# Chunk attention and a GELU feed-forward layer on one core: PSUM banks, AV order and an output copy at the seam between the first two tiles

## The chip, the core and the metric

The kernel runs on one core of one Trainium2 chip. The core has a matrix engine (TensorE, PE in the profile, with PEld for its weight loads), a vector engine (VectorE, DVE), an activation engine (ScalarE, ACT), a general engine (GpSimd, POOL) and SyncE (SP), which here issues nearly all DMAs. Each engine works through its own instructions in program order, and semaphores make one wait for another. Matmuls write to PSUM, which is handed out here as eight banks of 128 partitions x 512 float32.

The metric is the device time of one execution in microseconds (us), smaller is better. Times in the profile's views count from the first instruction of the profiled execution.

## What is computed

Attention within chunks of 64 tokens, for 8 batches, 8 heads, 576 tokens and 64 channels a head; its result, as 4608 rows of 512, goes through a layer 512 -> 2048 -> 512 with the exact GELU.

```
scores = scale * np.matmul(q_c, k_c.transpose(0, 1, 2, 4, 3))     # q_c, k_c, v_c: (8, 8, 9, 64, 64)
attn = np.exp(scores - max);  attn = attn / attn.sum(-1)
x = (attn @ v_c).transpose(0, 2, 1, 3).reshape(4608, 512)
h = x @ w_in                                                       # (4608, 2048)
g = 0.5 * h * (1.0 + erf(h / sqrt(2)))
out = g @ w_out                                                    # (4608, 512)
```

## The kernel before

**Tiles.** The 72 chunk positions are cut into nine tiles of 512 tokens (`NT = 9`): tiles 0 to 7 are the first 512 tokens of a batch each, tile 8 the last chunks of all batches. For each tile the kernel does attention, which leaves `x` (512 channels as four groups of 128 partitions, `G = 4`), then mm1 (`h_ps`, line 298: 16 groups f of four accumulating matmuls, one for each k slice `ks` = channel group of `x`, followed by a Gelu on ACT, line 301), then mm2 (`y_ps`, lines 314 and 349: four row blocks ms of 16 matmuls), whose results are copied to SBUF as `y_sb` (line 318) and written out by a DMA that SP issues (line 323 for tiles 0 to 7).

**Software pipeline.** The order is written by hand and kept (`manual_schedule`). While PE does mm1 and mm2 of tile t, the attention of tile t + 1 is put between, slot by slot, by the dictionaries `extra1` (before mm1 group f) and `extra2` (before mm2 slot s) that `phase` is given. One channel group g (two heads) of attention is: scores on PE and exp on ACT (`att_S`, `pT`); the sums of the exps and their reciprocals; AV, eight matmuls of 64 columns into `av_ps` (line 264); and on DVE the multiplication of `av_ps` by the spread reciprocals `rc` into `x[g]` (line 265).

**Reciprocals.** For tile 1 group 0 has its own path (`att_sum`, lines 200 to 209). Groups 1 to 3 go through `att_sums(1, 1)`: four matmuls (line 218), a transpose and a reciprocal on DVE (lines 221, 223), then 12 small copies on ACT (line 227, four for each g, into `rb`); `att_rc` then makes `rc` of one g from `rb` by a DVE transpose (line 234).

**Tile 0's mm2.** It goes by rows (`by_rows=True`): slots 0 to 11 do one f for all four row blocks at once (`mm2_rows`), so four `y_ps` banks are open: three from the pool `ps_mm` and, for ms = 3, one from `ps_at`. Slots 12 to 15 finish the row blocks ms = 0 to 3 in turn, four matmuls each (`mm2_slot`, qt = 3), and each is then copied to `y_sb`: ms 0 to 2 on ACT, ms 3 on DVE. After ms = 2 ACT loads the Gelu table. In these slots stand the sums of tile 1 (slot 12), AV 0 and `rc` 1 (slot 13), AV 1 and `rc` 2 (slot 15), and AV 2 and `rc` 3 at the end; AV 3 stands in mm1 of tile 1, before its k slice 1 (`between`, `last_av`).

**Tile 1's mm1.** `phase` starts mm1 of a tile with several groups at once (`first`, line 357: 2 for tile 0, 3 for tile 1, 1 for the others), k slice by k slice, so that a late `x[g]` holds up less. For tile 1 these are `h_ps` 0 to 2, all from `ps_mm`.

**Pools.** PSUM is split into `ps_mm` (3 banks: `h_ps`, `y_ps`), `ps_tp` (2) and `ps_at` (3: scores, sums, AV; and `y_ps` 3 of tile 0). For tile 1 AV 0 and 1 are in `ps_at`, AV 2 and 3 in `ps_tp`. A tile gets a bank when its former user is done with it; the banks are assigned when the program is built. `y_sb` has four buffers in turn.

**Queues.** In the loop over tiles, SP issues in program order: the outputs of tile t - 1 (as mm2 produces them), the two transposing DMAs of tile t + 1 (`flip`, line 163, q and k), for t = 1 also the eight v loads of tile 2 (line 129), then q, k and eight v loads of tile t + 2 (lines 112 and 129). POOL casts `v_bd` of tile t + 1 (line 137) and q and k of tile t + 2 (line 133).

Of the kernel before, what the change touches and what calls it, by code (L numbers as in the profile page):

```python
# [11 lines left out]
def kernel(  # L12
# [9 lines left out]
    nc = tc.nc  # L22
    P = 128
    f32 = mybir.dt.float32
    bf16 = mybir.dt.bfloat16
    Act = mybir.ActivationFunctionType

    B, H, S, D = q.shape
    CH = 64
# [3 lines left out]
    G = H // 2  # L33
    d_model = H * D
# [3 lines left out]
    MT = CT * CH  # L38
    NT = B + 1
# [31 lines left out]
    def zero_v(i, eng):  # L71
        eng.memset(v_bds[i][0:CH, :, :, CH:P], 0.0)
        eng.memset(v_bds[i][CH:P, :, :, 0:CH], 0.0)
# [17 lines left out]
    ypool = ctx.enter_context(tc.tile_pool(name="ypool", bufs=4))  # L91
    ps_mm = ctx.enter_context(tc.tile_pool(name="ps_mm", bufs=3, space=bass.MemoryType.PSUM))
    ps_tp = ctx.enter_context(tc.tile_pool(name="ps_tp", bufs=2, space=bass.MemoryType.PSUM))
    ps_at = ctx.enter_context(tc.tile_pool(name="ps_at", bufs=3, space=bass.MemoryType.PSUM))
# [3 lines left out]
    def stage_tile():  # L98
        return stage.tile([P, SW], f32, tag="stage", name="arrival")

    tiles = [dict() for _ in range(NT)]

    def load_qk(t, nm, h0=0, h1=H):

        st = tiles[t]
        src = q if nm == "q" else k
        if nm + "f" not in st:
            st[nm + "f"] = stage_tile()[:].rearrange("p (h j d) -> p h j d", h=H, j=J)
            st[nm] = ld.tile([P, G, J, 2, D], bf16, tag=nm, name=f"{nm}_nat")
        raw = st[nm + "f"]  # L110
        if t < B:
            nc.sync.dma_start(raw[:, h0:h1], src[t, h0:h1, 0:MT, :].rearrange("h (p j) d -> p h j d", j=J))  # L112
        else:
            for b in range(B):
                nc.sync.dma_start(
                    raw[PC * b:PC * (b + 1), h0:h1],
                    src[b, h0:h1, MT:S, :].rearrange("h (p j) d -> p h j d", j=J))
# [29 lines left out]
    def att_Tq(t, g, copy):  # L147
        tp = transposed(t, "q", g)
        qT = work.tile([P, CT, CH], bf16, tag="qT", name="qT", bufs=5)
        copy(qT[:].rearrange("p i (c j) -> p i c j", j=J), tp)  # L150
        tiles[t]["qT", g] = qT
# [59 lines left out]
            return rest_of_it  # L211
        rest_of_it()

    def att_sums(t, first=0):

        sum_ps = ps_at.tile([P, MT], f32, tag="at", name="sums_ps")
        for g in range(G):
            nc.tensor.matmul(sum_ps[QD * g:QD * (g + 1)], ones_c[:], tiles[t]["pT", g][:], start=True, stop=True,  # L218
                             tile_position=(0, QD * g))
        t1 = work.tile([P, NB, 32], f32, tag="t1", name="t1", bufs=2)  # L220
        nc.vector.transpose(t1[:], sum_ps[:].rearrange("p (n e) -> p n e", e=32))  # L221
        r1 = work.tile([P, 2, NB], f32, tag="r1", name="r1", bufs=2)
        nc.vector.reciprocal(r1[:], t1[:].rearrange("p n (r e) -> p r n e", r=2)[:, :, :, 0])  # L223
        rb = work.tile([P, G, NB], f32, tag="rb", name="rb", bufs=2)
        for g in range(first, G):
            for s in range(G):
                nc.scalar.copy(rb[QD * s:QD * (s + 1), g], r1[QD * g:QD * (g + 1), s // 2])  # L227
        tiles[t]["rb"] = rb

    def att_rc(t, g):  # L230

        rb = tiles[t]["rb"]
        rc = work.tile([P, NB, 32], f32, tag="rc", name="rc", bufs=4)
        nc.vector.transpose(rc[:], rb[:, g].to_broadcast([P, NB, 32]))  # L234
        tiles[t]["rc", g] = rc
# [34 lines left out]
    DV, AC, PO = nc.vector.tensor_copy, nc.scalar.copy, nc.gpsimd.tensor_copy  # L270

    def att_units(t, cq=DV, ck=DV):
        tiles[t]["x"] = xpool.tile([P, G, MT], bf16, tag="x", name="x")
        T = []
        for g in range(G):
            T += [lambda g=g: att_Tq(t, g, cq), lambda g=g: att_Tk(t, g, ck if t == 0 or g < 2 else DV)]
        S_ = [lambda g=g: att_S(t, g) for g in range(G)]
        if t > 1:
            T = [lambda g=g: flip_k(t, g, ck) for g in range(G)]
            S_ = [lambda g=g: att_S_flipped(t, g) for g in range(G)]  # L280
        if t > 0:
            U = [lambda: att_sums(t), *[lambda g=g: att_rc(t, g) for g in range(G)]]
        else:
            U = [lambda g=g: att_sum(t, g) for g in range(G)]
        A = [lambda g=g: att_av(t, g) for g in range(G)]
        return T, S_, U, A


    def mm1_slot(t, f, n=1, between={}):
        st = tiles[t]  # L290
        if f == 0:
            st["h"] = hpool.tile([P, FF, MT], bf16, tag="h", name="h")
        h_ps = [ps_mm.tile([P, MT], f32, tag="mm", name="h_ps") for _ in range(n)]
        for ks in range(KS):
            for u in between.get(ks, ()):
                u()
            for a in range(n):
                nc.tensor.matmul(h_ps[a][:], w_in_sb[:, ks, (f + a) * P:(f + a + 1) * P], st["x"][:, ks, :],  # L298
                                 start=(ks == 0), stop=(ks == KS - 1))
        for a in range(n):  # L300
            nc.scalar.activation(st["h"][:, f + a, :], h_ps[a][:], Act.Gelu)  # L301

    NQ = 4
    def mm2_slot(t, ms, qt):
        st = tiles[t]
        if t == NT - 1 and ms == MT // P - 1:
            if qt == 0:
                last_rows(t, ms)
            return
        if qt == 0:  # L310
            st["y_ps", ms] = ps_mm.tile([P, d_model], f32, tag="mm", name="y_ps")
        y_ps = st["y_ps", ms]
        for f in range(qt * FF // NQ, (qt + 1) * FF // NQ):
            nc.tensor.matmul(y_ps[:], st["h"][:, f, ms * P:(ms + 1) * P], w_out_sb[:, f, :],  # L314
                             start=(f == 0), stop=(f == FF - 1))
        if qt == NQ - 1:
            y_sb = ypool.tile([P, d_model], f32, tag="y", name="y_sb")
            (AC if t == 0 and ms < 3 or ms % 2 == 0 and t + 1 < NT else DV)(y_sb[:], y_ps[:])  # L318
            if t == 0 and ms == 2:
                act_table(Act.Gelu)  # L320
            if t < B:
                m0 = t * S + ms * P
                nc.sync.dma_start(out[m0:m0 + P, :], y_sb[:])
            else:
                for c in range(P // CH):
                    m0 = (ms * (P // CH) + c) * S + MT
                    nc.sync.dma_start(out[m0:m0 + CH, :], y_sb[c * CH:(c + 1) * CH, :])

    def last_rows(t, ms):
        h = d_model // 2  # L330
# [21 lines left out]
    def phase(t, extra1, extra2, by_rows=False, between={}):  # L352
        nms = MT // P
        order = [(ms, qt) for ms in range(nms) for qt in range(NQ)]
        if by_rows:
            order = [(None, f) for f in range(FF - FC)] + [(ms, NQ - 1) for ms in range(nms)]
        first = (2, 3, 1)[min(t, 2)]
        mm1_slot(t, 0, first, between)
        for f in range(first, FF):
            for u in extra1.get(f, ()):  # L360
                u()
            mm1_slot(t, f)
        for s, (ms, qt) in enumerate(order):
            for u in extra2.get(s, ()):
                u()
            if ms is None:
                mm2_rows(t, qt)
            else:
                mm2_slot(t, ms, qt)
        for u in extra2.get("end", ()):  # L370
            u()
# [40 lines left out]
    def act_table(func):  # L412
        nc.scalar.activation(act_scratch[:], rest[:, 0:1], func)  # L413

    with tc.manual_schedule():
# [9 lines left out]
        zero_v(0, nc.vector)  # L425
        T, S_, U, A = att_units(0, DV, AC)
        cast_qk(0, "k", 0, PO)
# [21 lines left out]
        cast_qk(0, "q", 3, DV)  # L449
        U[0]()  # L450
        T[5]()
        T[6]()
        T[7]()
        U[1]()
        S_[2]()
# [15 lines left out]
        wout = [load_w_out(0)]  # L471
# [31 lines left out]

        T, S_, U, A = att_units(1, AC, AC)
        def next_qk():
            for nm in "qk":
                load_qk(2, nm)
        phase(0, {}, {0: [lambda: act_table(Act.Exp)],
                      2: [T[0]], 3: [T[2]], 4: [T[4], T[6]], 7: [T[1], T[3]], 8: [T[5], S_[0]],
                      9: [T[7], S_[1], next_qk], 10: [S_[2], lambda: att_sum(1, 0), lambda: wout[3](2, DV)],  # L510
                      11: [lambda: wout[3](3, AC), S_[3]], 12: [lambda: att_sums(1, 1)],
                      13: [A[0], U[2]], 15: [A[1], U[3]], "end": [A[2], U[4]]},
              by_rows=True)
        last_av = {1: [A[3]]}
        pool_cast_qk(2)
        for t in range(1, NT):
            nxt = t + 1 < NT
            if nxt:
                T, S_, U, A = att_units(t + 1)
# [44 lines left out]
```

## Time and profile before

| | us |
|---|---|
| median of 6 runs (lowest to highest) | 294.9 (294.17 to 295.9) |
| the profiled execution | 295.0 |
| its span, first to last instruction | 293.2 |

Mean granted clock of TensorE in the profiled execution: 0.994.

| stretch of the profiled execution, us | length | PE busy | DVE busy | ACT busy | POOL busy |
|---|---|---|---|---|---|
| 46.2 to 55.0, the seam of tiles 0 and 1 | 8.8 | 8.06 | 6.52 | 6.23 | 6.67 |
| 54.8 to 82.3, the rest of tile 1 | 27.5 | 27.21 | 11.80 | 18.14 | 13.88 |
| 82.3 to 112.3, tile 2 | 30.0 | 29.79 | 12.81 | 18.94 | 9.39 |
| 112.3 to 142.3, tile 3 | 30.0 | 29.84 | 13.24 | 18.93 | 9.13 |

In the views below a timeline row reads: start, length from the first to the end of the last instruction in it, engine, line, operation, output <- inputs, shape, count, and in brackets how long the engine stood idle before it and what ended that. Rows of one engine can overlap a little, since an instruction starts before the one ahead of it has drained. "Issue" is time in which an engine waited for nothing that the profile shows.

### The profile page before, as it was taken

The page shows a single profiled execution, that of the slowest core. Times are in us where ns is not written, and L with a number is a line of the kernel's source. Part 1 is how long each engine was busy: PE and PEld are TensorE (multiplying, and loading weights), DVE is VectorE, ACT ScalarE, POOL GpSimd, SP SyncE. Part 2 cuts the span into 40 slices and gives each one's busy share as a digit, 9 for nine tenths or more (in the row PEclk, how much of TensorE's full clock was granted, in tenths as well). Part 3 has the DMA queues.
Part 4 walks back from the last instruction along what each step waited for, and adds up shares of the span by engine and source line. Part 5 has one row for each costly group of instructions (what it writes and reads, how often), then busy time and mean ns, then how long its engine had stood idle before and what let it go on. Part 6 is the DMA issues. An engine that isn't in the chain of part 4 may idle for free.

```text
span 293.2 us, 4862 instructions
## 1 busy us (share of the span) xinstructions
PE 282.3 (96%) x1845; PEld 139.0 (47%) x1880; DVE 125.4 (43%) x204; ACT 176.4 (60%) x376; POOL 98.3 (34%) x137
## 2 busy tenths in 40 slices
PE   7699999999999999999999999999999999999995
PEld 3354454445544454455445544554454445444444
DVE  6864348352806081608260725163246433550011
ACT  3757766776646774677378636863686368637400
POOL 7669758606632630281006400740002700000000
PEclk9889999999999999999999999999999999999999
DMA  7999998999869616971598149904999860020032
GB/s 220 230 366 403 397 316 247 308 218 311 228 174 323 166 46 163 317 167 72 141 288 217 61 131 291 237 36 131 178 133 143 247 143 2 36 91 19 0 72 72
DMA packets 96887, 53.79 MB, mean 183 GB/s; under 512 B 68576, under 2 KB 89312, under 8 KB 96864
## 3 DMA queue, kind: packets, MB, share of 16 engines
q1 hardware_dynamic: 96704, 53.36, 67.5%
q8 instruction: 14, 0.23, 0.3%
q10 hardware_dynamic: 160, 0.13, 0.2%
q14 instruction: 9, 0.07, 0.1%
HBM read 36.70 MB, written 9.44 MB: 157 GB/s over the span
## 4 chain that ended last, share of the span: by engine, by line
PE 84%; SPq 6%; DMA 3%; ACT 3%; issue 1%; DVE 1%; POOL 1%; POOLq 0%
PE h_ps L298 37%; PE y_ps L314 35%; PE y_ps L349 3%; PE av_ps L264 3%; SPq L129 3%; DMA arrival<-in_k_dram 2%; PE s_ps L180 2%; SPq L112 2%; SPq L163 1%; PE y_ps L334 1%; DMA arrival<-in_v_dram 1%; ACT rb L227 1%; PE sums_ps L218 1%; ACT k_bd L157 1%; PE tp L144 1%
## 5 line engine op out<-in xcount | busy, mean ns | idle before, releaser
L298 PE MATMUL h_ps<-x,w_in_sb 128*128 128x512 bf16 x565 | 125.9, 379 | 1.3 <-ACT h L301 0.3
L301 ACT ACTIVATE h<-h_ps 128x512 bf16<-128x512 f32 x144 | 85.7, 597 | 62.2 <-PE h_ps L298 62.1
L314 PE MATMUL y_ps<-w_out_sb,h 128*128 128x512 bf16 x492 | 118.9, 379 | 0.9
L298 PEld LDWEIGHTS <-w_in_sb 128*128 128x128 bf16 x576 | 56.2, 98 | 68.3 <-issue 1.2
L314 PEld LDWEIGHTS <-h 128*128 128x128 bf16 x512 | 45.4, 98 | 46.7 <-issue 1.8
L172 DVE COPY k_bd<-k_t 64x512 bf16<-64x512 bf16 x56 | 35.0, 624 | 49.6 <-DMA k_t<-k_nat 48.5
L133 POOL CAST q_nat<-arrival 128x512 bf16<-128x512 f32 x31 | 19.8, 676 | 96.8 <-DMA arrival<-in_q_dram 96.8
L137 POOL CAST v_bd<-arrival 64x512 bf16<-64x512 f32 (+1 forms) x30 | 36.6, 1219 | 18.1 <-DMA arrival<-in_v_dram 11.8
L227 ACT COPY rb<-r 32x16 f32<-32x16 f32 x124 | 25.0, 201 | 16.1 <-DVE r L223 14.5
L318 DVE COPY y_sb<-y_ps 128x512 f32<-128x512 f32 x18 | 12.3, 685 | 36.6 <-PE y_ps L314 36.6
L265 DVE TENSOR_TENSOR x<-av_ps,rc 128x512 bf16<-128x512 f32 x36 | 24.7, 690 | 4.3 <-PE av_ps L264 0.8
L221 DVE STREAM_TRANSPOSE t<-sums_ps 128x512 f32<-128x512 f32 x8 | 5.7, 717 | 46.6 <-PE sums_ps L218 46.6
L133 POOL CAST k_nat<-arrival 128x512 bf16<-128x512 f32 x34 | 20.1, 630 | 15.0 <-DMA arrival<-in_k_dram 9.6
L234 DVE STREAM_TRANSPOSE rc<-rb 128x512 f32<-128x512 f32 x31 | 21.8, 704 | 6.6 <-ACT rb L227 6.6
L413 ACT ACT_TABLE_LOAD x18 | 23.1, 1283 | 1.0 <-PEq L548 0.7
L264 PEld LDWEIGHTS <-v_bd 128*128 128x128 bf16 x288 | 13.2, 99 | 8.2 <-issue 0.6
L318 ACT COPY y_sb<-y_ps 128x512 f32<-128x512 f32 x17 | 9.8, 587 | 8.4 <-PE y_ps L314 8.3
L183 ACT ACTIVATE pT<-s_ps 128x512 bf16<-128x512 f32 x28 | 14.7, 591 | 0.0
L264 PE MATMUL av_ps<-pT,v_bd 128*128 128x64 bf16 x288 | 14.5, 194 | 0.2
L180 PEld LDWEIGHTS <-k_bd 128*128 128x128 bf16 x224 | 10.4, 98 | 6.6
L349 PE MATMUL y_ps<-w_out_sb,h 128*128 128x512 bf16 x46 | 11.9, 379 | 0.4 <-ACT h L301 0.3
L180 PE MATMUL s_ps<-q_t,k_bd 128*128 128x64 bf16 x224 | 11.1, 193 | 0.0
(62 smaller groups left out, 117.1 us busy)
## 6 DMA issues: line engine op xcount, KB each, us to landing
arrival<-in_v_dram SPq DMA_DIRECT2D x72, 128.0 KB, 4.2
out_dram<-y_sb SPq DMA_DIRECT2D x32, 256.0 KB, 2.2
arrival<-in_q_dram SPq DMA_DIRECT2D x7, 1024.0 KB, 6.2
arrival<-in_k_dram SPq DMA_DIRECT2D x7, 1024.0 KB, 9.1
arrival<-in_moe_w_out_dram SPq DMA_DIRECT2D x4, 1024.0 KB, 12.3
arrival<-in_moe_w_in_dram SPq DMA_DIRECT2D x4, 512.0 KB, 5.8
arrival<-in_moe_w_in_dram SPq DMA_DIRECT2D x2, 1024.0 KB, 9.9
arrival<-in_q_dram SPq DMA_DIRECT2D x4, 256.0 KB, 4.6
```

What stands on the lines that cost most here:

```text
L133: copy(st[nm][:, g].rearrange("p j r d -> p r j d"), st[nm + "f"][:, 2 * g:2 * g + 2])
L137: copy(v_bds[t % NV][sl, :, gs, sl].rearrange("p i g d -> p g i d"), tiles[t]["vf"][sl, gs])
L172: copy(k_bds[g][sl, :, sl].rearrange("p i (c j) -> p i c j", j=J), src[sl])
L180: nc.tensor.matmul(s_ps[:, i, :].rearrange("p (j c) -> p j c", j=J), k_bds[g][:, i, :], qt[:, i], start=True, stop=True)
L227: nc.scalar.copy(rb[QD * s:QD * (s + 1), g], r1[QD * g:QD * (g + 1), s // 2])
L264: nc.tensor.matmul(av_ps[:, i, :], v_bds[t % NV][:, i, g, :], st["pT", g][:, i, :], start=True, stop=True)
L265: nc.vector.tensor_tensor(st["x"][:, g, :], av_ps[:].rearrange("p i e -> p (i e)"), st["rc", g][:].rearrange("p n e -> p (n e)"), op=mybir ...
L298: nc.tensor.matmul(h_ps[a][:], w_in_sb[:, ks, (f + a) * P:(f + a + 1) * P], st["x"][:, ks, :], start=(ks == 0), stop=(ks == KS - 1))
L301: nc.scalar.activation(st["h"][:, f + a, :], h_ps[a][:], Act.Gelu)
L314: nc.tensor.matmul(y_ps[:], st["h"][:, f, ms * P:(ms + 1) * P], w_out_sb[:, f, :], start=(f == 0), stop=(f == FF - 1))
L318: (AC if t == 0 and ms < 3 or ms % 2 == 0 and t + 1 < NT else DV)(y_sb[:], y_ps[:])
L413: nc.scalar.activation(act_scratch[:], rest[:, 0:1], func)
```

## The change

Four things are changed, all at the seam between tile 0's mm2 and tile 1's mm1:

- The first mm1 step of tile 1 takes its second and third `h_ps` from `ps_at` (`mm1_slot`); the first stays in `ps_mm`.
- AV 1 and `rc` 2 move from slot 15 to slot 14, AV 2 and `rc` 3 from the end to slot 15.
- `att_sums` no longer makes the `rb` copies; it returns `over(g)`, which makes the four of one g. For tile 1 those of g = 1 stand in slot 12, before the copy of `y_ps` 0, and those of g = 2 and 3 in slot 13, behind it. Tiles 2 to 8 still make all 16 at once.
- The copy-out is a function of its own (`rows_out`). For tile 0's last row block it is no longer called in slot 15 but next to AV 3, in mm1 of tile 1. The copy on DVE thus stands behind the last multiplication into `x`, and its DMA on SP behind all the loads that the loop's first pass issues (transposes of tile 2, v of tile 2, q, k and v of tile 3).

```diff
-    def att_sums(t, first=0):
+    def att_sums(t):
...
         rb = work.tile([P, G, NB], f32, tag="rb", name="rb", bufs=2)
-        for g in range(first, G):
+        tiles[t]["rb"] = rb
+
+        def over(g):
             for s in range(G):
                 nc.scalar.copy(rb[QD * s:QD * (s + 1), g], r1[QD * g:QD * (g + 1), s // 2])
-        tiles[t]["rb"] = rb
+        return over
...
-            U = [lambda: att_sums(t), *[lambda g=g: att_rc(t, g) for g in range(G)]]
+            U = [lambda: [over(g) for over in [att_sums(t)] for g in range(G)], *[lambda g=g: att_rc(t, g) for g in range(G)]]
...
-        h_ps = [ps_mm.tile([P, MT], f32, tag="mm", name="h_ps") for _ in range(n)]
+        banks = [(ps_mm, "mm")] + [(ps_at, "at") if t == 1 else (ps_mm, "mm")] * (n - 1)
+        h_ps = [pool.tile([P, MT], f32, tag=tag, name="h_ps") for pool, tag in banks]
...
         if qt == NQ - 1:
-            y_sb = ypool.tile([P, d_model], f32, tag="y", name="y_sb")
-            (AC if t == 0 and ms < 3 or ms % 2 == 0 and t + 1 < NT else DV)(y_sb[:], y_ps[:])
...
+            if t > 0 or ms < 3:
+                rows_out(t, ms)
+
+    def rows_out(t, ms):
+        y_ps = tiles[t]["y_ps", ms]
+        y_sb = ypool.tile([P, d_model], f32, tag="y", name="y_sb")
+        (AC if t == 0 and ms < 3 or ms % 2 == 0 and t + 1 < NT else DV)(y_sb[:], y_ps[:])
...
+        over = []
+
+        def sums():
+            over.append(att_sums(1))
+            over[0](1)
         phase(0, {}, {0: [lambda: act_table(Act.Exp)],
...
-                      11: [lambda: wout[3](3, AC), S_[3]], 12: [lambda: att_sums(1, 1)],
-                      13: [A[0], U[2]], 15: [A[1], U[3]], "end": [A[2], U[4]]},
+                      11: [lambda: wout[3](3, AC), S_[3]], 12: [sums],
+                      13: [A[0], lambda: over[0](2), lambda: over[0](3), U[2]], 14: [A[1], U[3]], 15: [A[2], U[4]]},
               by_rows=True)
-        last_av = {1: [A[3]]}
+        last_av = {1: [A[3], lambda: rows_out(0, 3)]}
```

More of the change, by code (lines that the diff above doesn't have):

```diff
@@ L316, in mm2_slot @@
         if qt == NQ - 1:
-            y_sb = ypool.tile([P, d_model], f32, tag="y", name="y_sb")
[L318 to L327, printed above, removed]
+            if t > 0 or ms < 3:
[4 more added lines that the diff above has]
+        (AC if t == 0 and ms < 3 or ms % 2 == 0 and t + 1 < NT else DV)(y_sb[:], y_ps[:])
+        if t == 0 and ms == 2:
+            act_table(Act.Gelu)
+        if t < B:
+            m0 = t * S + ms * P
+            nc.sync.dma_start(out[m0:m0 + P, :], y_sb[:])
+        else:
+            for c in range(P // CH):
+                m0 = (ms * (P // CH) + c) * S + MT
+                nc.sync.dma_start(out[m0:m0 + CH, :], y_sb[c * CH:(c + 1) * CH, :])
     def last_rows(t, ms):
```

## The prediction

> **What bounds the kernel now.** I read the page's busy shares and slices first. TensorE (PE) works 96% of the span and from the third slice on is at 9 tenths in every slice but the last; the granted clock is at 9 tenths or more from the fourth on. So only time in which PE stands still can be won.
>
> ```profile
> PE 282.3 (96%) x1845; PEld 139.0 (47%) x1880; DVE 125.4 (43%) x204; ACT 176.4 (60%) x376; POOL 98.3 (34%) x137
> PE   7699999999999999999999999999999999999995
> ```
>
> Next the chain of waits, cut to the seam between tile 0's mm2 and tile 1's mm1 (columns: start, length, what). It leaves PE and passes through ScalarE's (ACT) copies of `y_ps`, then through a Gelu.
>
> ```profile
> 50.46 1.57 ACT y_sb L318 x3
> 52.08 0.38 PE h_ps L298
> 54.23 0.61 ACT h L301
> 54.88 1.24 PE h_ps L298 x5
> ```
>
> The timeline there shows what PE does. The AV group that starts at 50.49 is 8 matmuls that take 0.22 us before the next may start (47.43 to 47.66 at the first AV of this seam, earlier in the same view); a 512-column matmul takes 0.216 (below, the 64 of tile 2: 13.98 less 0.38, over 63 steps).
>
> ```profile
> 48.74 0.71 DVE L234 STREAM_TRANSPOSE rc<-rb 128x512 f32<-128x512 f32 x1 [0.19 <-ACT rb L227]
> 49.83 0.69 DVE L265 TENSOR_TENSOR x<-av_ps,rc 128x512 bf16<-128x512 f32 x1 [0.37 <-PE av_ps L264]
> 50.43 0.70 DVE L234 STREAM_TRANSPOSE rc<-rb 128x512 f32<-128x512 f32 x1
> 50.49 0.40 PE L264 MATMUL av_ps<-pT,v_bd 128*128 128x64 bf16 x8
> 51.06 0.65 DVE L318 COPY y_sb<-y_ps 128x512 f32<-128x512 f32 x1
> 51.10 1.35 PE L298 MATMUL h_ps<-x,w_in_sb 128*128 128x512 bf16 x3 [0.21 <-ACT y_sb L318]
> 52.52 2.11 PE L298 MATMUL h_ps<-x,w_in_sb 128*128 128x512 bf16 x9
> 53.05 0.69 DVE L265 TENSOR_TENSOR x<-av_ps,rc 128x512 bf16<-128x512 f32 x1
> 54.88 3.40 PE L298 MATMUL h_ps<-x,w_in_sb 128*128 128x512 bf16 x14 [0.25 <-ACT h L301]
> ```
>
> PE could go on at 50.71 (50.49 + 0.22) and starts at 51.10: 0.39 idle. The three first matmuls start at 51.10, 51.59 and 52.08 (the weight loads that follow each start then), some 0.04 after an ACT copy ends, at 51.05, 51.57 and 52.03: twice 0.27 idle. The nine that start at 52.52 are issued by 54.47, the next group starts at 54.88, when the first Gelu has freed a bank: 0.41 idle. Together **1.34 us** of idle PE. From 54.88 on PE is full: tile periods are 30.0 us (mm1 of later tiles starts at 82.22 and 112.31 in the chain), against 29.8 of PE work in such a window.
>
> **The change, part by part.**
>
> *Banks.* `h_ps` 1 and 2 of tile 1 take banks of `ps_at`: in the program as built those of AV 0 and AV 1, which their multiplications into `x` free. The groups f = 3 and 4 then take the `y_ps` 1 and 2 banks and no longer wait for a Gelu. Of all these, only `y_ps` 0 must be copied before mm1 starts, and that copy moves ahead of the last eight `rb` copies.
>
> *ACT.* Nothing is added, the order changes. `rb` copies start at 47.87 and take 0.214 each (2.57 for 12), a `y_sb` copy 0.52 (1.57 for 3). So: `rb` of g = 1 until 48.73, `y_sb` 0 until 49.25, `rb` of g = 2 until 50.11 and g = 3 until 50.96, `y_sb` 1 and 2 until 52.01, where it was 52.03. Then the table load, 1.28, and the 0.20 scratch activation: Gelus are possible from 53.5.
>
> *DVE.* The `y_sb` 3 copy (0.6 of DVE's time) goes from between to behind the `x` chain. Independent DVE operations start 0.61 apart (50.43, 51.06), and one that needs the one before 0.80 apart (52.25 to 53.05). `rc` 1 stays at 48.74; `x` 1 at 49.54, no longer kept to 49.83 by AV 1, which now runs from 48.51; `rc` 2 at 50.15 (its `rb` is done at 50.11, so it just fits); `x` 2 at 50.95; `rc` 3 at 51.56; `x` 3 at 52.36, done at 53.05 where it was 53.74: 0.69 earlier. The `y_sb` 3 copy runs from 52.97 to 53.6, with nobody behind it on DVE until `k_bd` at 62.16.
>
> *PE.* Same matmuls in another order. From 46.56: `y` 0 (4 x 0.216), AV 0 at 47.43, `y` 1, AV 1 at 48.51, `y` 2, AV 2 at 49.60, `y` 3, then mm1. AV 2 is the one that comes early for its data: GpSimd's (POOL) eight `v_bd` casts run from 45.36 to 50.94, about 0.67 apart, so that of g = 2 ends at 49.59 and AV 2's weights, which in this pattern are loaded 0.22 ahead, wait until then: 0 to 0.25 of stall, I take 0.15. mm1 starts at 50.84; three matmuls, AV 3 (v cast long done), six matmuls: the last k slice could start at 53.0. `x` 3 is there at 53.05 plus 0.04 of signalling (54.84 to 54.88 in the chain): 53.09. So the stall of AV 2 is covered by `x` 3's wait, and f = 3 starts at 53.09 + 3 x 0.216 = **53.74** instead of 54.88: **1.14 us** earlier. Its `y_ps` 1 bank is free at 51.5. The first Gelu starts at 53.5 and ends at 54.1; f = 5 needs its bank at 55.47; the one after f = 3 ends at 55.8 and f = 6 needs it at 56.3. No new wait there.
>
> A rule speaks against that last point: the Trainium skill, "ScalarE: Activation LUTs", section "What ACT_TABLE_LOAD costs", has a switch cost a drain on top of the load, 2.66 us in all. By it the first Gelu would start at 54.7, f = 6 would wait 0.7 us for its bank, and the sum would be 294.6. The rows below say otherwise: from the load's start at 66.92 to the next activation 1.40 us pass, and the sum goes by these.
>
> ```profile
> 66.92 1.28 ACT L413 ACT_TABLE_LOAD   x1
> 68.32 2.10 ACT L183 ACTIVATE pT<-s_ps 128x512 bf16<-128x512 f32 x4
> ```
>
> *Queues.* On SP, the DMA of `y_sb` 3 goes behind tile 2's two transposes and eight v loads and tile 3's q, k and eight v loads. What it was ahead of moves up at most; but the q transpose (54.04) waits for POOL's q casts, which end at 53.86, so it stays. The DMA itself is now issued at 77.3, after the last v load, ahead of tile 1's outputs, which stood there anyway (77.27): four issues of 0.35 become five. `y_sb` has four buffers, so tile 1's last copy now waits for that DMA to land: 77.3 + 0.35 + 2.2 (the page's median) = 79.9, wanted at 81.3 (82.42 less 1.14). Cover 1.4 us.
>
> *A side effect.* In the program as built, mm1 of tile 2 goes over two banks in turn, not three, for its first eight groups; the third is held for tile 1's last output. So group f waits for Gelu f - 2:
>
> ```profile
> 82.22 13.98 PE L298 MATMUL h_ps<-x,w_in_sb 128*128 128x512 bf16 x63
> 83.28 0.60 ACT L301 ACTIVATE h<-h_ps 128x512 bf16<-128x512 f32 x1 [3.73 <-PE h_ps L298]
> ```
>
> A group's Gelu ends 1.06 + 0.60 = 1.66 after its start, with 0.04 of signalling 1.70; the bank is wanted after 8 x 0.216 = 1.73. It fits by 0.03. If each wait costs another hop of 0.05, the three pairs cost 0.15. I take 0.05, between 0 and 0.15.
>
> *What is late next.* Tile 2's v cast: POOL 66.96 to 70.83; AV 0 of tile 2 loads weights at 72.44, now 71.30. 0.47 us of slack. The `k_bd` copies end at 67.11 and their last user (69.18) comes at 68.0.
>
> ```profile
> 66.96 3.87 POOL L137 CAST v_bd<-arrival 64x2048 bf16<-64x2048 f32 x2 [8.92 <-DMA arrival<-in_v_dram]
> 72.44 0.49 PEld L264 LDWEIGHTS <-v_bd 128*128 128x128 bf16 x8
> ```
>
> **Sum.** -1.14 + 0.05 = -1.09. The profiled execution took 295.0 (span 293.2 and 1.8 around it), so 293.9; the median shown is 294.9, 0.1 lower, so **293.8**. The unknowns move it by 0.2 down (if `x` 3 binds nothing and all 1.34 is won) and 0.3 up (AV 2's stall longer, the two banks at 0.15).
>
> **Rivals.**
>
> *Only the banks help.* If the `x` chain is not pulled in, `x` 3 stays at 53.74 and the last k slice starts at 53.78: f = 3 at 54.43, 0.45 won, 294.45. For it: `rc` 2 fits behind its `rb` by 0.04, and ACT now has a `y_sb` copy ahead of that `rb`; any delay on ACT goes straight into `x` 3. Against: ACT showed no wait in its twelve `rb` and three `y_sb` copies, and the data of `y_ps` 0 is there at 47.8, well before 48.73.
>
> *Slower: tile 2's v comes late.* Place: SP's eight v loads at 59.89, which took 5.38 us to issue; tile 3's took 10.55 (66.62), because each waits for an earlier transfer. If the moved output shifts the queue slots so that tile 2's take 10.55 too, the cast ends 5.2 later, at 76.0, and AV 0 waits 4.7: 1.1 won, 4.7 lost, 298.5. It decides from 0.47 of delay, and outweighs the gain from 1.6. For it: DMA is at 9 tenths or more in that stretch. Against: the change takes 256 KB out of the way before those loads and adds none.
>
> *It does all and more.* All the idle time goes: 1.34, 293.6. That is inside the forecast's range.
>
> **How the numbers follow.** A measurement of this kernel tells from no change about 0.3%, 0.9 us, so "faster" is below 294.0. The forecast has 0.75, and 0.10 of this ends above 294.0, by the unknowns and the scatter of the medians (294.17 to 295.9 in six runs). The first rival has 0.17, the second 0.08. So faster 0.65, within 0.3% 0.27, slower 0.08. The forecast's own range is 293.4 to 294.2; widened by some 0.2 of scatter below, and above to take in the first rival with its scatter, 293.2 to 294.9.
>
> **What would show it.** f = 3 of tile 1 starts 1.1 us earlier against the end of tile 0's sums; mm1's first three matmuls start 0.22 apart; no matmul waits for an ACT copy at the seam; `x` 3 about 0.7 earlier; tile 2's mm1 is still 13.98 us for 64 matmuls; later tiles keep their 30.0 us period. Wrong it would be if tile 2's mm1 is stretched, if tile 2's AV 0 waits for POOL, or if `x` 3 comes no earlier.

## The result and the profile after

| | median, us (lowest to highest) | runs |
|---|---|---|
| before | 295.32 (294.17 to 298.86) | 74 |
| after | 294.41 (293.09 to 295.77) | 37 |

The ratio of after to before is 0.9964, with a 95% interval of 0.9953 to 0.9975: 1.06 us won (0.74 to 1.39 of 295.32). It is worked out from all the runs; the two medians alone differ by 0.91. Forecast were 1.09 us, 293.8 and a range of 293.2 to 294.9.

The profiled execution of after took 294.84 us, span 292.9, granted clock 1.000. That is only 0.3 less span than before's 293.2, and the spans alone would mislead. So every trace is cut at the same places of the program, and the pieces are compared:

- **start**: from the span's start to the first of tile 1's sums (line 218), the last PE work that stands in both kernels at the same place
- **seam**: from there to the start of tile 1's mm1 group f = 3, where PE was full again in before. Where that group begins inside a row, its start is the row's start and the matmuls ahead of it, 0.216 us each: in after the last k slice starts at 53.93, three matmuls later it is 54.58, and 54.58 less 46.93 is 7.65
- **rest of tile 1**: from f = 3 to tile 2's mm1
- **the other tiles**: from there to the start of the last half block of mm2

| | start | seam | rest of tile 1 | other tiles |
|---|---|---|---|---|
| before | 46.23 | 8.65 | 27.34 | 203.75 |
| after | 46.93 | 7.65 | 27.33 | 203.76 |
| difference | +0.70 | -1.00 | -0.01 | +0.01 |

The whole gain is in the seam, and 0.70 of it is covered in this one trace by a later start. In 13 traces of this study the start lies anywhere from 45.24 to 47.60, though the change and the experiments (but e8) leave the instructions ahead of it as they are. In after tile 0's mm1 already began 0.41 later than in before (18.63 against 18.22) and waited again at 19.19 for a cast of `w_in`, that is for loads; where the rest of the 0.70 arose was not followed. Many runs average over the start, and their ratio gives 1.06.

The busy shares and slices of after's page show no more than that:

```profile
PE 280.4 (96%) x1846; PEld 137.7 (47%) x1880; DVE 125.7 (43%) x204; ACT 176.3 (60%) x376; POOL 99.2 (34%) x137
PE   6589999999999999999999999999999999999995
```

PE's first three slices are emptier than before's 7, 6, 9: the later start. The seam, at 46 to 55 us, is in the seventh and eighth slices, which read 9 in both; a slice is too coarse for 1 us. The chain of waits (start, length, what) shows it:

```profile
50.30 0.69 DVE x L267
50.99 0.69 DVE rc L236
...
51.77 0.69 DVE x L267
52.46 0.63 DVE rc L236
...
53.19 0.70 DVE x L267
...
53.93 2.10 PE h_ps L301 x9
```

Before, the chain went through ACT's three `y_sb` copies and a Gelu. Both are gone; what ends last now is DVE's row of `rc` and `x`, up to `x` 3. The timeline of after at the seam:

```profile
46.93 0.40 PE L218 MATMUL sums_ps<-pT,ones_c 128*32 128x512 bf16 x4
...
49.48 0.59 ACT L326 COPY y_sb<-y_ps 128x512 f32<-128x512 f32 x1
...
50.09 1.70 ACT L229 COPY rb<-r 32x16 f32<-32x16 f32 x8
...
51.42 0.81 PE L301 MATMUL h_ps<-x,w_in_sb 128*128 128x512 bf16 x3
...
52.90 1.28 ACT L421 ACT_TABLE_LOAD   x1
...
53.79 0.68 DVE L326 COPY y_sb<-y_ps 128x512 f32<-128x512 f32 x1
53.93 2.32 PE L301 MATMUL h_ps<-x,w_in_sb 128*128 128x512 bf16 x10 [0.17 <-DVE x L267]
...
54.34 2.06 ACT L304 ACTIVATE h<-h_ps 128x512 bf16<-128x512 f32 x4
```

mm1's first three matmuls take 0.81 us in one piece, where they were spread over 1.35. There is one wait of PE left: the row at 53.93. PE could have started that k slice 0.33 earlier (the six matmuls ahead start at 52.30 and take 0.216 each, to 53.60); the bracket shows 0.17 of it, since in this view the last matmul ahead ends only at 53.76.

### The profile page after: what moved, and what is told of

The parts are those of the page before. It is cut to its first block, busy times and chain, and to the rows that moved or that the text cites. A ratio compares the mean times of both kernels' runs of the same rounds, so it can differ in the third digit from the quotient of the medians.

```text
span 292.9 us, 4864 instructions
## 1 busy us (share of the span) xinstructions
PE 280.4 (96%) x1846; PEld 137.7 (47%) x1880; DVE 125.7 (43%) x204; ACT 176.3 (60%) x376; POOL 99.2 (34%) x137
## 4 chain that ended last, share of the span: by engine, by line
PE 88%; SPq 4%; DVE 3%; DMA 2%; issue 1%; ACT 1%; POOL 0%; DVEq 0%; POOLq 0%
PE h_ps L301 42%; PE y_ps L317 36%; SPq L129 3%; PE y_ps L357 3%; PE av_ps L266 2%; PE s_ps L180 2%; DMA arrival<-in_moe_w_in_dram 2%; SPq L112 1%; PE y_ps L342 1%; PE sums_ps L218 1%; DVE x L267 1%; DVE rc L236 1%; PE tp L144 1%; POOL w_in_sb L397 0%; ACT k_bd L157 0%
```

## The experiments

The ratio is to before, from runs of before on the same chip; seam and rest of tile 1 are from the kernel's one trace. The last column is when GpSimd's cast of tile 2's v starts, counted from f = 3.

| kernel | ratio (95%) | start | seam | rest of tile 1 | v cast |
|---|---|---|---|---|---|
| before | 1 | 46.23 | 8.65 | 27.34 | 12.08 |
| after | 0.9964 (0.9953 to 0.9975) | 46.93 | 7.65 | 27.33 | 13.10 |
| after, again | 0.9975 (0.9953 to 0.9996) | 47.60 | 7.61 | 27.34 | 13.55 |
| e1, banks only | 1.0006 (0.9978 to 1.0035) | 46.40 | 8.22 | 27.34 | 12.19 |
| e2, no banks | 1.0017 (0.9994 to 1.004) | 46.76 | 8.78 | 27.85 | 14.37 |
| e3, copy in place | 1.0002 (0.9979 to 1.0025) | 46.58 | 8.00 | 27.43 | 13.96 |
| e4, AVs late | 0.9969 (0.993 to 1.0008) | 46.53 | 7.82 | 27.33 | 13.69 |
| e5, faster `x` chain | 0.9974 (0.9958 to 0.9991) | 45.24 | 7.35 | 27.34 | 13.82 |
| e6, e5 with Gelus in order | 0.9962 (0.9939 to 0.9984) | 46.08 | 7.54 | 27.34 | 13.15 |
| e7, e5 with AV 2 later | 0.9944 (0.9923 to 0.9964) | 46.23 | 7.32 | 27.34 | 13.58 |
| e7, again | 0.9955 (0.993 to 0.9981) | 46.99 | 7.32 | 27.77 | 14.30 |
| e8, e7 with v loads early | 1.0142 (1.0108 to 1.0176) | 46.80 | 7.31 | 34.02 | early |
| e9, e7 with Gelus in order | 0.9953 (0.9925 to 0.998) | 47.27 | 7.32 | 27.35 | 13.32 |

The other tiles take 203.75 or 203.76 in all of them. Since one step is worth some tenths of a microsecond and the start scatters by 2, the traces' pieces decide between theories; the ratios say whether the whole agrees.

### e1_banks_only: before with the other banks, nothing else

```diff
-        h_ps = [ps_mm.tile([P, MT], f32, tag="mm", name="h_ps") for _ in range(n)]
+        banks = [(ps_mm, "mm")] + [(ps_at, "at") if t == 1 else (ps_mm, "mm")] * (n - 1)
+        h_ps = [pool.tile([P, MT], f32, tag=tag, name="h_ps") for pool, tag in banks]
```

> The kernel before with one part of the change alone: h_ps 1 and 2 of tile 1's first mm1 step from ps_at. Measure: the seam, from the start of tile 1's sums matmuls (line 218) to the start of mm1 group f = 3 of tile 1; 8.65 us before (46.23 to 54.88), 7.65 after (46.93 to 54.58). My theory: mm1 starts once y_ps 0 is copied, its matmuls run 0.22 apart, f = 3 no longer waits for a Gelu, but the last k slice then waits for x 3, which comes 7.51 us after the sums as before: seam 8.2, total 0.45 us less than before. Rival, the banks are the whole gain: seam 7.65, total 1.0 less.

The seam took 8.22 us, 0.43 less than before. The timeline of e1:

```profile
53.97 3.40 PE L299 MATMUL h_ps<-x,w_in_sb 128*128 128x512 bf16 x15 [0.37 <-DVE x L265]
```

With two of the three banks free early, PE comes sooner to its last k slice and then waits for `x` 3, which is as late as before (6.84 us after the sums, 6.83 before). The banks alone win 0.43; the rest of the 1.34 us of idle time turns into a wait for DVE. The total can't show 0.43: its interval holds both no change and that gain.

### e2_no_banks: after with the old banks

```diff
-        banks = [(ps_mm, "mm")] + [(ps_at, "at") if t == 1 else (ps_mm, "mm")] * (n - 1)
+        banks = [(ps_mm, "mm")] + [(ps_mm, "mm")] * (n - 1)
```

> The changed kernel with h_ps 1 and 2 taken from ps_mm again; AV order, rb order and the late output copy stay. My theory: x 3 comes as early as after (7.0 us after the sums), but nobody can use it: h_ps 1 and 2 wait for the y_ps 1 and 2 copies and f = 3 for the first Gelu. Seam 8.8 us, total 0 to 0.2 us more than before. Rival, the earlier x chain is what gains, with or without the banks: seam 8.0 to 8.2, total 0.5 less than before.

The timeline of e2 at the seam:

```profile
52.25 0.86 PE L301 MATMUL h_ps<-x,w_in_sb 128*128 128x512 bf16 x2 [0.35 <-ACT y_sb L326]
...
55.54 1.67 PE L301 MATMUL h_ps<-x,w_in_sb 128*128 128x512 bf16 x7 [0.25 <-ACT h L304]
```

Those are the two waits of before, for a `y_sb` copy and for a Gelu, and the seam is 8.78 long, no better than before. So the early `x` chain is worth nothing without the banks, and the banks without it 0.43; together they give 1.00. AV 2 also waited 0.24 here for its `v_bd` cast. That isn't what makes the seam long: mm1's second group waits for the `y_sb` 1 copy, which ACT does right behind its `rb` copies, from 51.61. Tile 2's AV 0 waited for its cast too, which made the rest of tile 1 0.51 longer; more on that at e7_again.

### e3_copy_in_place: after, with the last output copied where it was

```diff
-            if t > 0 or ms < 3:
-                rows_out(t, ms)
+            rows_out(t, ms)
...
-        last_av = {1: [A[3], lambda: rows_out(0, 3)]}
+        last_av = {1: [A[3]]}
```

> The changed kernel with tile 0's last output block copied out in slot 15 as before, so ahead of x 3 on DVE and with its DMA ahead of the transposes on SP. My theory: DVE does rc 3, y_sb 3, x 3 instead of rc 3, x 3: x 3 starts 6.66 us after the sums instead of 6.26, f = 3 0.4 later: seam 8.05, total 0.6 less than before. Rival, the place of the copy doesn't matter because PE is bound elsewhere: seam 7.65, total 1.0 less. If the DMA's place on SP matters, tile 2's v cast (67.68 after, with 0.6 us of slack) or tile 2's mm1 moves.

The seam took 8.00, 0.35 longer than after's. The timeline of e3 shows the copy between `rc` 3 (52.00, not shown) and `x` 3:

```profile
52.62 0.65 DVE L325 COPY y_sb<-y_ps 128x512 f32<-128x512 f32 x1
53.20 0.67 DVE L267 TENSOR_TENSOR x<-av_ps,rc 128x512 bf16<-128x512 f32 x1
```

In after `x` 3 follows `rc` 3 by 0.81 (52.38 to 53.19), here by 1.20. The difference is less than the copy's 0.6, since the copy fills the 0.2 that DVE otherwise spends between an operation and the one that needs it. That puts the last part of the change, the copy's new place, at 0.35 to 0.4 us. The total (1.0002) doesn't show that this kernel's seam is 0.65 shorter than before's. In the trace 0.09 of that is lost again in the rest of tile 1, and the 0.56 that is left lies just within the interval.

### e4_av_late: after, with AV 1 and 2 in their old slots

```diff
-                      13: [A[0], lambda: over[0](2), lambda: over[0](3), U[2]], 14: [A[1], U[3]], 15: [A[2], U[4]]},
+                      13: [A[0], lambda: over[0](2), lambda: over[0](3), U[2]], 15: [A[1], U[3]], "end": [A[2], U[4]]},
```

> The changed kernel with AV 1 and rc 2 back in slot 15 and AV 2 and rc 3 back at the end. My theory: AV 1 is done 3.6 us after the sums, so x 1 starts 0.2 later and all of the x chain with it: seam 7.9, total 0.75 less than before. Rival, x 1 waits for its rc and not for AV 1, and AV 2 no longer comes close to its v cast: seam 7.65, total 1.0 less.

The seam took 7.82: `x` 1 waits for AV 1 and the chain behind it is 0.2 late. The timeline of e4:

```profile
50.13 0.69 DVE L267 TENSOR_TENSOR x<-av_ps,rc 128x512 bf16<-128x512 f32 x1 [0.37 <-PE av_ps L266]
```

So the slots are worth 0.17 to 0.21 (against 7.65 and 7.61). The other part of the change, the split of the `rb` copies, was not taken back alone. With all twelve ahead of the `y_sb` 0 copy mm1 starts 4.87 us after the sums (e1), with the split 4.50 (after); what that is worth by itself is not shown.

### e5_x_chain_faster: all `rb` copies first, other banks, another order of Gelus

What still binds in after is `x` 3. Here ACT makes all twelve `rb` copies before any `y_sb` copy. So that mm1 need not wait for the copies, its first two groups take the banks of `ps_at` and only the third that of `y_ps` 0; the third's Gelu goes first. `rc` 3 is moved ahead of AV 2.

```diff
-        banks = [(ps_mm, "mm")] + [(ps_at, "at") if t == 1 else (ps_mm, "mm")] * (n - 1)
+        banks = [(ps_at, "at") if t == 1 and a < n - 1 else (ps_mm, "mm") for a in range(n)]
...
-        for a in range(n):
+        for a in ((2, 0, 1) if n == 3 else range(n)):
...
-            over[0](1)
+            for g in range(1, G):
+                over[0](g)
...
-                      13: [A[0], lambda: over[0](2), lambda: over[0](3), U[2]], 14: [A[1], U[3]], 15: [A[2], U[4]]},
+                      13: [A[0], U[2]], 14: [A[1], U[3], U[4]], 15: [A[2]]},
```

> The changed kernel with x 3 made earlier still: all 12 rb copies at once, ahead of the y_sb 0 copy; rc 3 on DVE before x 2, so that no operation of the chain follows directly on the one it needs; h_ps 0 and 1 from ps_at and h_ps 2 from ps_mm, so that y_ps 0 may be copied later; and of the first three Gelus that of group 2 first, whose ps_mm bank f = 5 needs. My theory: what is left of the idle time after the change is the wait of the last k slice for x 3 (0.33 us in its trace); x 3 is done 6.5 us after the sums, before PE wants it at 6.66. Seam 7.31 us instead of 7.65, total 0.33 less than after, 1.35 less than before (ratio to before 0.9954). Rival, that idle time moves to another wait (h_ps 1 for x 1, h_ps 2 for the y_ps 0 copy, f = 5 for its Gelu): seam 7.6, total as after.

The seam took 7.35, 0.30 less than after's. The low span of this trace, 290.9, is mostly its start, the earliest of all; the ratio, 0.9974, is that of after's repeat in the same comparison, 0.9975. A gain of 0.3 us is within those intervals, so the totals neither show nor exclude it.

### e6_gelu_in_order: e5 with the Gelus as in after

```diff
-        for a in ((2, 0, 1) if n == 3 else range(n)):
+        for a in range(n):
```

> As e5_x_chain_faster, with the Gelus in order 0, 1, 2. My theory: f = 3 starts at the same place (seam 7.31), but the third Gelu ends some 9.1 us after the sums, when f = 5 already wants its bank at 9.04: PE idles about 0.1 us there. Rival: the Gelu table is ready late enough that the wait is longer, up to 0.6 us, and the gain of e5 is gone.

The seam took 7.54, but not because of the Gelus: AV 2 waited 0.22 for its `v_bd` cast, as in e2. So this run says nothing on the order of the Gelus; e9 does.

### after_again

> The changed kernel as it is, in the same call, for the comparison: seam 7.65 us, ratio to before 0.996 to 0.997. From the start of f = 3 to the start of the last half block (line 342) 231.25 us, as in the traces of before and after, where both have 231.25.

The seam took 7.61, and the ratio's interval overlaps that of the first comparison. The start, 47.60, is the latest of all, so its profiled time, 295.58, lies above before's median in spite of the gain.

### e7_av2_after_y3: e5 with AV 2 behind the last output row

```diff
-                      13: [A[0], U[2]], 14: [A[1], U[3], U[4]], 15: [A[2]]},
+                      13: [A[0], U[2]], 14: [A[1], U[3], U[4]], "end": [A[2]]},
```

> As e5_x_chain_faster, with AV 2 back behind tile 0's last four matmuls instead of ahead of them. In the traces of e2_no_banks and e6_gelu_in_order AV 2 waited 0.26 and 0.22 us for its v cast; in e5 it came 0.02 late. My theory: here AV 2 is wanted 0.86 us later and never waits, x 2 still comes in time: seam 7.3 to 7.4 us whatever the casts do, the rest of tile 1 as in e5. Rival, AV 2 late makes x 2 and x 3 late: seam 7.6 or more.

Where AV 2 stands 0.86 later, its cast is done in time in every trace (e7, its repeat, e8 and e9). The timeline of e7:

```profile
50.73 0.81 PE L301 MATMUL h_ps<-x,w_in_sb 128*128 128x512 bf16 x3
...
51.40 1.28 DVE L267 TENSOR_TENSOR x<-av_ps,rc 128x512 bf16<-128x512 f32 x2
...
51.61 4.70 PE L301 MATMUL h_ps<-x,w_in_sb 128*128 128x512 bf16 x21
```

`x` 2 and `x` 3 are done at 52.68, before PE comes to the last k slice, and no matmul waits any more. The seam is 7.32, 1.33 less than before's: all the idle time that was counted in before's seam. By chance this trace has before's start to the hundredth, 46.23, and its span is 1.3 less, 291.9 against 293.2. The ratio, 0.9944, is the lowest of the study.

### e8_v_load_early: e7 with tile 2's v loaded before its transposes

```diff
         def next_qk():
             for nm in "qk":
                 load_qk(2, nm)
+            load_v(2)
...
-                if t == 1:
-                    load_v(2)
```

> As e7_av2_after_y3, with the eight v loads of tile 2 issued behind tile 2's q and k loads in mm2 of tile 0, some 12 us earlier, instead of behind the two transposes. From f = 3 of tile 1 to mm1 of tile 2 takes 27.34 us where tile 2's v cast is in time, 27.43 and 27.85 in e3 and e2, where AV 0 of tile 2 waited for it. My theory: the v cast of tile 2 comes 3 us or more earlier, so its slack is no longer eaten by what the seam gains; 27.34, total the same as e7 or up to 0.2 us less in the median. Rival: the 1 MB of v takes DMA time from q and k of tile 2 and from the transposes; k_t lands later and the scores of tile 2 wait for k_bd: more than 27.4.

The cast of v started at 60.36 and bound nothing any more, but the kernel was 1.4% slower than before: the scores of tile 2 waited for `k_bd`, as the rival had it. The timeline of e8:

```profile
67.94 2.42 DVE L172 COPY k_bd<-k_t 64x512 bf16<-64x512 bf16 x4 [14.11 <-DMA k_t<-k_nat]
69.17 0.45 PEld L180 LDWEIGHTS <-k_bd 128*128 128x128 bf16 x8 [4.17 <-DVE k_bd L172]
69.18 0.61 PE L180 MATMUL s_ps<-q_t,k_bd 128*128 128x64 bf16 x8 [3.68 <-DVE k_bd L172]
```

In e7 the same copies start at 62.27. There SP issues k's transposing DMA at 58.41, here at 64.02: it stands behind the eight v loads, which took SP from 47.90 to 58.75 to issue, and the outputs. POOL's k casts, which that DMA needs too, end only 0.4 later after the sums than in e7, so most of the delay is the order in SP's queue and not, as the rival had it, the DMA time that v takes. PE stands still for 3.68 us, and runs slowly afterwards. Busy time in stretches of e8 (columns: stretch, length, PE, PEld, DVE, ACT and POOL busy, granted clock, DMA share, GB/s):

```profile
65.40:69.10 3.70, 0.10 (x1) 0.00 (x0) 1.15 (x2) 2.08 (x3) 0.00 (x0) 0.88 0.92 240
69.10:72.00 2.90, 2.74 (x20) 1.60 (x22) 2.78 (x6) 0.64 (x2) 0.05 (x1) 0.50 1.06 359
72.00:76.00 4.00, 3.86 (x26) 1.89 (x26) 1.13 (x2) 1.41 (x3) 3.69 (x6) 0.62 1.15 320
76.00:80.00 4.00, 3.95 (x35) 1.93 (x35) 1.19 (x3) 1.86 (x7) 2.30 (x4) 1.00 0.83 237
...
68.00:69.00 1.00, 0.00 (x0) 0.00 (x0) 0.99 (x2) 0.00 (x0) 0.00 (x0) 0.61 0.91 298
```

The rest of tile 1 is 6.68 us longer than e7's: 3.68 of idle time and 3.0 of half-speed matmuls. The row behind the dots is a part of the wait, used in the last section. So the order of transposes before v in SP's queue must stay; the v cast has to be got earlier in another way.

### e9_gelu_in_order: e7 with the Gelus as in after

The edit is e6's, on e7.

> As e7_av2_after_y3, with the first three Gelus of tile 1 in the order 0, 1, 2. In e6_gelu_in_order AV 2's wait had hidden what this order costs. My theory: the third Gelu ends 9.05 us after the sums, just when f = 5 wants its bank: 0 to 0.1 us of idle PE there, total the same as e7 within 0.1. Rival: a stall of 0.3 us or more before f = 5, mm1 of tile 2 that much later.

Seam 7.32, rest of tile 1 27.35: the order of the three Gelus costs at most 0.01 in this trace. The edit isn't needed; the copies and the table load are done early enough for either order.

### e7_again

> e7_av2_after_y3 once more, for a second interval: seam 7.3 us, 27.34 from f = 3 to mm1 of tile 2, ratio to before 0.9955 (1.33 us less), between 0.994 and 0.997 as measured.

The seam repeated, 7.32; the rest of tile 1, expected at 27.34, did not. The timeline of this run:

```profile
68.61 3.84 POOL L137 CAST v_bd<-arrival 64x2048 bf16<-64x2048 f32 x2 [9.03 <-DMA arrival<-in_v_dram]
...
72.50 0.41 PE L266 MATMUL av_ps<-pT,v_bd 128*128 128x64 bf16 x8 [0.25 <-POOL v_bd L137]
```

Tile 2's AV 0 waits for the cast of v, which waited for v's DMA. AV 0 comes 17.77 us after f = 3 where nothing holds it (72.34 in after, below), here 18.19: 0.43 lost. The cast takes 3.84 and some hundredths of signalling, so it binds from a start of about 13.87 after f = 3. The table agrees: nothing is lost at 13.82 (e5), 0.1 at 13.96 (e3), 0.43 and 0.51 at 14.30 and 14.37. Counted from the sums instead, the cast starts at 20.4 to 23.2 in all kernels but e8, whatever the seam. Most of the traces put its wait down to v's DMA (e3 and e5 to PE's scores). So, as far as these traces go, each tenth won at the seam comes off its slack. With the 0.43 lost, the seam and the rest of tile 1 take 35.09 together in this run, no less than after's 34.98.

## Why the prediction came out right, point by point

**1.34 us of idle PE at the seam.** Shown: e7 takes it all away, and the seam shortens by 1.33.

**f = 3 comes 1.14 us earlier.** Mis-sized: 1.00 in after's trace, 1.05 in the repeat. The mechanism is as forecast, the last k slice waits for `x` 3, but `x` 3 starts 6.26 after the sums, not 6.13 (before: 6.82). So it comes 0.56 earlier and not 0.69. Of these 0.13, 0.04 come from the transpose of the sums: it starts 0.56 after them where before it took 0.50, and hands most of that on (in the repeat it isn't late, and `x` 3 starts at 6.22). Another 0.05 is `rc` 2, which was to fit behind its `rb` by 0.04 and did not: the `y_sb` 0 copy held ACT from 49.48 to 50.09, 0.61, where 0.52 had been taken from a row of three such copies back to back. That edge was named as the forecast's weak place; its price was less than a tenth of the 0.69 that the rival gave it. The rest is DVE's step between dependent operations, up to 0.82 and not 0.80. (The pair named for the step of independent ones, 50.43 and 51.06, is 0.63 apart; the 0.61 is that from 51.64 to 52.25.)

**AV 2 stalls 0.15 (0 to 0.25) for its cast.** It was 0 in both traces of after, 0.24 in e2 and 0.22 in e6, which have it in the same slot: the bounds were right, and the stall comes and goes from run to run. In after it would be hidden by `x` 3's wait, as forecast; in e6, where that is gone, it costs its full length.

**The last output out of DVE's chain.** The forecast counted 0.6 of DVE's time as moved away; e3 shows the end of the chain 0.35 to 0.4 earlier by it. (The 1.14 didn't rest on the 0.6: it was added up from the steps of the chain.) The DMA's new place on SP cost nothing. These rows of after's timeline show it, with what follows:

```profile
67.68 3.84 POOL L137 CAST v_bd<-arrival 64x2048 bf16<-64x2048 f32 x2 [8.70 <-DMA arrival<-in_v_dram]
...
72.34 0.40 PE L266 MATMUL av_ps<-pT,v_bd 128*128 128x64 bf16 x8
...
78.88 4.28 SPq L331 DMA_DIRECT2D out_dram<-y_sb  x5
...
82.11 0.69 DVE L326 COPY y_sb<-y_ps 128x512 f32<-128x512 f32 x1 [2.10 <-PE y_ps L317]
```

The five issues start behind tile 3's last v load, as forecast, 0.9 later after the sums than forecast (78.88 less 46.93 against 77.3 less 46.23). Tile 1's last copy, which reuses that DMA's buffer, waited for PE only. But the cover of 1.4 us was not there: the DMA landed at 81.80, 0.31 before the copy. In the repeat and in e4, e5, e6, e9 and e7's repeat the copy waited for the DMA to land, and PE lost nothing by it: the other tiles take 203.75 there as well.

**No new wait at the Gelus.** Right: the first Gelu in after's timeline starts 1.44 us behind the table load's start (52.90 to 54.34). By the 2.66 of the Trainium skill ("ScalarE: Activation LUTs", "What ACT_TABLE_LOAD costs") it would have been 55.56; the measurement decides against it here.

**Two banks in turn in tile 2's mm1, 0.05 (0 to 0.15).** Nothing: its 64 matmuls take 13.98 as before, and the other tiles 203.76 against 203.75.

**The sum.** -1.00 at the seam and 0.00 for the two banks, where -1.14 and +0.05 were forecast; the runs give -1.06 (-0.74 to -1.39). The absolute time, 294.41, missed 293.8 by 0.6. Of this 0.42 is what it was counted from: the six runs shown had a median of 294.9, all 74 of before 295.32. The other 0.18 is the difference of the medians, 0.91 and not 1.09. So 294.41 lies outside the forecast's own 293.4 to 294.2, above the 294.0 that was to mean "faster", and within the stated range only because that was widened for the first rival, whose 294.45 it nearly meets. By the absolute time alone the hit would be luck. The ratio tells the two apart (the rival's 0.45 us lies outside 0.74 to 1.39), and so do the pieces of the traces.

**The rivals.** *Only the banks help* is kernel e1, which gained 0.43 at the seam against the rival's 0.45; after is not that kernel. *Tile 2's v comes late* is real, and much smaller than feared: in after the cast starts 0.77 before it would bind (13.10 against 13.87), in the repeat 0.32, and in e2, e3 and e7's repeat it did bind, by 0.1 to 0.5. The moved output didn't change how the loads queue: tile 2's eight took 5.38 us to issue in before and in after. Why tile 3's take about twice that is open; that each waits for an earlier transfer is not shown. What the forecast didn't see is that the slack moves from run to run: by 0.7 between the two traces of e7, and, counted from the sums, by 2.7 over the kernels that load v in the same order. *It does all and more* took two further edits (e5 and e7).

**A version that is better.** e7, or e9, which is e7 without the new order of Gelus, has 0.33 less seam than after. Against before they measure 0.9944, 0.9955 and 0.9953; their intervals overlap after's 0.9964, so the 0.33 is shown by the traces and not yet by the totals. And in e7's repeat the cast of v took all of it back.

## What to carry to other kernels

Two causes that hold one place in turn must both be removed: here banks alone won 0.43, the early chain alone nothing, both 1.00. When a step is worth less than the scatter of a run, cut the traces at fixed instructions and compare the pieces. Before loads are moved ahead in a queue, see who stands behind them: in e8 a cover of tenths was bought with a wait of 3.7 us and a slowed clock after it.

## What the runs showed of the hardware that was not expected

- In e8's wait of 3.68 us without matmuls (65.50 to 69.18) PE's granted clock fell to 0.50 some 2.7 us in (1.00 from 67 to 68, 0.61 on average from 68 to 69). It stayed there for about 6 us of work: 0.50 from 69.10 to 72.00, 0.62 on average to 76.00, then 1.00. The Trainium skill ("TensorE: Matmul & The Clock Gate", "What's actually happening") has half speed after an idle window of about 3.4 us and full speed after some 3.4 us of sustained work. The 0.50 agrees with e8's rows; there the clock fell somewhat sooner, and the slow stretch was longer.
- A DVE cast of 128x512 float32 to bf16 just before the sums' transpose took 0.39 us in before, 0.51 in e7 and 0.82 in after, with POOL casts of v running beside it in each.
- Two DVE operations of 0.69 us start 0.61 apart where they are independent and 0.80 to 0.82 apart where the second needs the first; a copy put between costs the chain only 0.39 (e3, 1.20 against 0.81 in after).
